# Layer 1 and q computed with the weights as the moving operand in four column groups, w1 in one transfer, GELU's polynomial on GpSimd

## The chip, the cores and the metric

One core of a Trainium2 chip runs the whole kernel. The metric is the device time of one execution in microseconds (us), median of several runs. The execution times quoted are of the fast state unless a state is named. The profiler reports a span, from the first to the last recorded instruction of the kernel. The timed figure is longer than the span, and the difference between the two is "timed minus span". Spans of single runs are known to 0.1 us, so such a difference carries 0.05 us of rounding; for a profiled run the trace has the span to the nanosecond. In the views of the profile, PE is TensorE and PEld its weight loads, DVE is VectorE, ACT ScalarE, POOL GpSimd and SP SyncE. In rows of forty digits, each digit is the busy share of a fortieth of the span, in tenths.

## The reference, cut to what matters

One token, two branches and a gate. All inputs are bfloat16.

```python
q = x @ wq                                  # 576 -> 32 heads x 128
k, v = last 4096 keys of each of 16 caches  # 16 x 4096 x 128 each, 2 heads per cache
a = softmax(q k / sqrt(128)) v @ wo         # -> 576
h = gelu_tanh(x @ w1 + b1)                  # 576 -> 4608
b = h @ w2 + b2                             # -> 576
g = sigmoid(sum(x * gate_w))
out = g * a + (1 - g) * b
```

Some 53.6 MB must be read, most of it k and v, and each byte is used once.

Of the kernel before, what the change touches and what calls it, by code (L numbers as in the profile page):

```python
# [9 lines left out]
FP32 = mybir.dt.float32  # L10
BF16 = mybir.dt.bfloat16
I32 = mybir.dt.int32
ACT = mybir.ActivationFunctionType
ALU = mybir.AluOpType
# [4 lines left out]
def kernel(  # L19
# [15 lines left out]
    nc = tc.nc  # L35

    P = 128
    D = 576
    Hq, Hkv, Dh = 32, 16, 128
# [7 lines left out]
    FH = F // 2  # L47
    NJ = FH // P
    NF = 2 * NJ
    NI = 2 * D // P  # L50
    QH = Hq * Dh // 2
    DH = D // 2
# [153 lines left out]
    const = ctx.enter_context(tc.tile_pool(name="const", bufs=1))  # L206
    big = ctx.enter_context(tc.tile_pool(name="big", bufs=1, side="right"))
    kt_pool = ctx.enter_context(tc.tile_pool(name="kt_pool", bufs=2, side="right"))
    ps_s = ctx.enter_context(tc.tile_pool(name="ps_s", bufs=2, space=bass.MemoryType.PSUM))
    ps_y = ctx.enter_context(tc.tile_pool(name="ps_y", bufs=1, space=bass.MemoryType.PSUM))  # L210
    ps_m = ctx.enter_context(tc.tile_pool(name="ps_m", bufs=2, space=bass.MemoryType.PSUM))


    rows = kt_pool.tile([2, 8192], BF16, name="rows", tag="kt")
    x_row = rows[0:1, 0:D]
    gw_row = rows[0:1, D : 2 * D]
    b2_row = rows[0:1, 2 * D : 3 * D]
    b1_t = rows[0:2, 3 * D : 3 * D + FH]
    xdup = rows[0:1, 3 * D + FH : 5 * D + FH]
    junk_row = rows[0:1, 5 * D + FH : 6 * D + FH]  # L220
# [5 lines left out]

    w1_t = big.tile([P, NI, FH], BF16, name="w1_t", tag="B")
    w1_src = B_w1.rearrange("d (h n) -> (d h) n", h=2).rearrange("(p i) n -> p i n", i=NI)
    for i0, i1 in ((0, 4), (4, NI)):
        nc.sync.dma_start(out=w1_t[:, i0:i1, :], in_=w1_src[:, i0:i1, :])  # L230
    wq_t = big.tile([P, NI, QH], BF16, name="wq_t", tag="A")
    wq_src = A_wq.rearrange("d (h n) -> (d h) n", h=2).rearrange("(p i) n -> p i n", i=NI)
# [10 lines left out]
    for base, pattern, keep in (  # L243
# [13 lines left out]
        out=is0[:], in0=low[:], scalar1=0.0, scalar2=None, op0=ALU.is_equal  # L257
    )
    alt = is0[:, 0 : 2 * NI].rearrange("p (i t) -> p i t", t=2)
    ones = const.tile([P, P], FP32, name="ones")  # L260
    nc.gpsimd.memset(ones[:], 1.0)
    ident = const.tile([P, P], BF16, name="ident")
    make_identity(nc, ident[:])
    RW = 31
    NZ = 512 + 5 * RW + 1 + 64
    zeros = const.tile([P, NZ + 4 * D], BF16, name="zeros")
    nc.gpsimd.memset(zeros[:].bitcast(FP32), 0.0)
    perm = zeros[:, 0:512].rearrange("p (j b l) -> p j b l", j=4, b=4)
    at31 = zeros[:, 512 : 512 + 5 * RW].rearrange("p (a r) -> p a r", a=5)
# [3 lines left out]
        out=perm,  # L273
        in_=perm,
        pattern=[[-64, 2], [-1, 2], [0, 4], [-2, 32]],
        compare_op=ALU.not_equal,
        fill=1.0,
        base=0,
        channel_multiplier=1,
    )  # L280
    nc.gpsimd.affine_select(
        out=at31,
        in_=at31,
        pattern=[[-RW, 5], [-1, RW]],
        compare_op=ALU.not_equal,
        fill=1.0,
        base=0,
        channel_multiplier=1,
# [3 lines left out]
        out=hi5[:],  # L292
        in_=ones[:, 0:5],
        pattern=[[-RW, 5]],
        compare_op=ALU.is_ge,
        fill=0.0,
        base=0,
        channel_multiplier=1,
    )
    nc.gpsimd.affine_select(  # L300
        out=hi5[:],
        in_=hi5[:],
        pattern=[[RW, 5]],
        compare_op=ALU.is_ge,
        fill=0.0,
        base=RW - 1,
        channel_multiplier=-1,
# [4 lines left out]
        out=hi16[:], in0=is0[:, c0 : c0 + 16], scalar1=-SCALE, scalar2=None, op0=ALU.mult  # L312
# [5 lines left out]
        out=row_of[:],  # L318
        in_=row_of[:],
        pattern=[[0, 16], [-1, HB], [0, 2]],  # L320
        compare_op=ALU.not_equal,
        fill=1.0,
        base=0,
        channel_multiplier=1,
# [4 lines left out]
        out=foreign[:],  # L329
        in_=foreign[:],  # L330
        pattern=[[0, P], [-1, HB]],
        compare_op=ALU.not_equal,
        fill=0.0,
        base=0,
        channel_multiplier=1,
# [4 lines left out]
        out=xdup.rearrange("p (d t) -> p d t", t=2),  # L340
        in_=x_row.rearrange("p (d o) -> p d o", o=1).to_broadcast([1, D, 2]),
    )
    xs_ps = ps_m.tile([P, NI, 1], FP32, name="xs_ps", tag="m")
    for i in range(NI):
        nc.tensor.matmul(  # L345
            xs_ps[:, i, :],
            lhsT=xdup[:, i : 2 * D : NI],
            rhs=one_b[0:1, 0:1],
            start=(i == 0),
            stop=(i == NI - 1),  # L350
            skip_group_check=True,
        )
    x2 = const.tile([P, NI, 2], BF16, name="x2")
    nc.vector.tensor_tensor(
        out=x2[:], in0=xs_ps[:].to_broadcast([P, NI, 2]), in1=alt, op=ALU.mult
    )


# [2 lines left out]
        out=junk_row,  # L361
        in0=x_row,
        in1=gw_row,
        scale=1.0,
        scalar=0.0,
        op0=ALU.mult,
        op1=ALU.add,
# [9 lines left out]
    omg = const.tile([P, 1], FP32, name="omg")  # L377
    nc.vector.tensor_scalar(
        out=omg[:], in0=g_t[:], scalar1=-1.0, scalar2=1.0, op0=ALU.mult, op1=ALU.add
    )  # L380
    b2g = const.tile([1, D], FP32, name="b2g")
    nc.vector.tensor_scalar(
        out=b2g[:], in0=b2_row, scalar1=omg[0:1, 0:1], scalar2=None, op0=ALU.mult
    )
    gh = const.tile([P, 1, 5], FP32, name="gh")
# [1 line left out]
        out=gh[:, 0, :], in0=hi5[:], scalar1=g_t[:, 0:1], scalar2=None, op0=ALU.mult  # L387
# [18 lines left out]
    y_add(ones[0:1, 0:1], b2g[0:1, :], start=True)  # L406


    h_ps = ps_m.tile([P, NF], FP32, name="h_ps", tag="m")
    for j in range(NJ):  # L410
        nc.tensor.matmul(
            h_ps[:, j:NF:NJ],
            lhsT=b1_t[:, j:FH:NJ],
            rhs=ident[0:2, 0:2],
            start=(j == 0),
            stop=False,
            skip_group_check=True,
        )
    QZ = 24
    qz_flat = const.tile([P, QZ + 4 * NG * P + 96], BF16, name="qz_flat")  # L420
    nc.gpsimd.memset(qz_flat[:].bitcast(FP32), 0.0)
    for i in range(NI):
        for j in range(NJ):
            nc.tensor.matmul(  # L424
                h_ps[:, j:NF:NJ],
                lhsT=w1_t[:, i, j:FH:NJ],
                rhs=x2[:, i, :],
                start=False,
                stop=(i == NI - 1 and j == NJ - 1),
                skip_group_check=True,  # L430
            )
    hacc = const.tile([P, NF], FP32, name="hacc")
    nc.vector.tensor_copy(out=hacc[:], in_=h_ps[:])  # L433
    z2 = const.tile([P, NF], FP32, name="z2")
    nc.vector.tensor_tensor(out=z2[:], in0=hacc[:], in1=hacc[:], op=ALU.mult)
    C0 = 0.7978845608028654
    poly = const.tile([P, NF], FP32, name="poly")
    nc.vector.tensor_scalar(
        out=poly[:],
        in0=z2[:],  # L440
        scalar1=2.0 * C0 * 0.044715,
# [2 lines left out]
        op1=ALU.add,  # L444
    )
    u_t = const.tile([P, NF], FP32, name="u_t")
    nc.vector.tensor_tensor(out=u_t[:], in0=poly[:], in1=hacc[:], op=ALU.mult)
    e_h = const.tile([P, NF], FP32, name="e_h")
    nc.scalar.activation(out=e_h[:], in_=u_t[:], func=ACT.Exp, scale=-1.0)
    nc.vector.tensor_scalar(out=e_h[:], in0=e_h[:], scalar1=1.0, scalar2=None, op0=ALU.add)  # L450
# [1 line left out]
    nc.vector.reciprocal(out=r_t[:], in_=e_h[:])  # L452
    gt = const.tile([P, NF], BF16, name="gt")
    nc.vector.scalar_tensor_tensor(
        out=gt[:], in0=hacc[:], scalar=omg[:, 0:1], in1=r_t[:], op0=ALU.mult, op1=ALU.mult
    )


    q_ps = ps_m.tile([P, Hq], FP32, name="q_ps", tag="m")
    for i in range(NI):  # L460
        for j in range(Hq // 2):
            nc.tensor.matmul(  # L462
                q_ps[:, j : Hq : Hq // 2],
                lhsT=wq_t[:, i, j * Dh : (j + 1) * Dh],
                rhs=x2[:, i, :],
                start=(i == 0 and j == 0),
                stop=(i == NI - 1 and j == Hq // 2 - 1),
                skip_group_check=True,
            )
    q_b = const.tile([P, Hq], BF16, name="q_b")  # L470
    nc.scalar.copy(out=q_b[:], in_=q_ps[:])
    qj_ps = ps_m.tile([P, 4, NG, 8], FP32, name="qj_ps", tag="m")
    for j in range(4):
        nc.tensor.matmul(
# [293 lines left out]
```

## The kernel before: the parts that the change and the argument touch

All large loads go through SyncE's queue in the order in which they are needed; x, the gate's weights and the two biases, 1 to 9 KB each, go through ScalarE's queue. Two large weights come first, and their buffers are then used again for k, w2 and v.

```python
x_row = rows[0:1, 0:D]
...
b2_row = rows[0:1, 2 * D : 3 * D]
...
w1_t = big.tile([P, NI, FH], BF16, name="w1_t", tag="B")      # NI = 9, FH = 2304
for i0, i1 in ((0, 4), (4, NI)):
    nc.sync.dma_start(out=w1_t[:, i0:i1, :], in_=w1_src[:, i0:i1, :])
wq_t = big.tile([P, NI, QH], BF16, name="wq_t", tag="A")
...                                                            # one transfer
```

In layer 1 and q the weights are the fixed operand: each product first loads a block of 128 x 128 weights and then moves two columns of x past it, which leaves the result spread over 128 partitions.

```python
for i in range(NI):
    for j in range(NJ):                                        # 9 x 18 = 162
        nc.tensor.matmul(h_ps[:, j:NF:NJ], lhsT=w1_t[:, i, j:FH:NJ], rhs=x2[:, i, :], ...)
hacc = const.tile([P, NF], FP32, name="hacc")
nc.vector.tensor_copy(out=hacc[:], in_=h_ps[:])
... # z2 = hacc^2, poly = c1 z2 + c0, u = poly hacc on VectorE, exp on ScalarE,
... # then 1/(1 + e) and the product with (1 - g) on VectorE
for i in range(NI):
    for j in range(Hq // 2):                                   # 9 x 16 = 144
        nc.tensor.matmul(q_ps[:, j : Hq : Hq // 2], lhsT=wq_t[:, i, j * Dh : (j + 1) * Dh],
                         rhs=x2[:, i, :], ...)
nc.scalar.copy(out=q_b[:], in_=q_ps[:])
```

After that come four groups of k (load, transpose on VectorE, scores on TensorE, softmax), four of v, and the two output projections, whose products end the kernel.

## Time and profile before

| | before |
|---|---|
| time, median (lowest to highest of the first three) | 131.68 us (131.63 to 131.78) |
| span of the profiled run | 130.11 us |
| that run's time minus its span | 131.53 - 130.11 = 1.42 us |
| DMA queue, share of 16 engines | 96.5% |
| TensorE, VectorE, GpSimd busy | 79.7, 52.3, 9.2 us |
| last weight packet ends at | 127.50 us |
| instructions as built: TensorE, VectorE, GpSimd | 2211, 60, 47 |

The table says that the transfers fill the span and that the engines do not. The prediction below shows the lines that carry this. This is the start in order of time in the kernel before (start, duration, engine, line, operation, and in brackets how long the engine had been idle and what ended that):

```profile
6.09 0.75 DVE L339 COPY rows<-rows 1x1152 bf16<-1x1152 bf16 x1 [6.09 <-DMA rows<-in_A_x_dram]
7.67 0.75 DVE L360 CUSTOM_DVE_ANT_0 rows<-rows 1x576 bf16<-1x576 bf16 x1 [0.83 <-DMA rows<-in_gate_w_dram]
10.49 1.28 PE L411 MATMUL h_ps<-ident,rows 2*128 2x2 bf16 x18 [1.36 <-DMA rows<-in_B_b_dram]
24.16 0.20 DVE L433 COPY hacc<-h_ps 128x36 f32<-128x36 f32 x1 [11.91 <-PE h_ps L424]
27.00 4.00 PE L462 MATMUL q_ps<-x,wq_t 128*128 128x2 bf16 x144 [2.87 <-DMA wq_t<-in_A_wq_dram]
36.69 4.45 DVE L531 STREAM_TRANSPOSE kt<-k_t 128x4096 f32<-128x4096 f32 x1 [10.47 <-DMA k_t<-in_A_k_cache_dram]
```

The three small inputs x, gate and b1 were there by 6.1, 7.7 and 10.5 us. Layer 1 was summed at 24.16, q's products ran from 27.00, and the first k landed at 36.69.

### The profile page before, as it was taken

How to read it: one execution, taken by the hardware profiler on the slowest of the kernel's cores; microseconds unless marked ns; L12 is line 12 of the kernel's file. 1: busy time of each engine (PE TensorE's matmuls, PEld its weight loads, DVE VectorE, ACT ScalarE, POOL GpSimd, SP SyncE). 2: the span in 40 equal slices, each digit the busy share in tenths (PEclk: the TensorE clock that was granted, in tenths of full speed). 3: DMA queues.
4: the chain of work that ended last, by engine and by line, in shares of the span. 5: the costliest groups of instructions: out<-in, count | busy, mean ns of one | idle time of the engine just before them, and what ended most of it. 6: DMA issues, size and time to landing. Idle time of an engine off the chain costs nothing.

```text
span 130.1 us, 2403 instructions
## 1 busy us (share of the span) xinstructions
PE 79.7 (61%) x1148; PEld 45.6 (35%) x1077; DVE 52.3 (40%) x48; ACT 8.3 (6%) x18; POOL 9.2 (7%) x26
## 2 busy tenths in 40 slices
PE   0037999476003998939918994995300830899573
PEld 0037679375000121201211120595300830855441
DVE  0153000400079959999999995614000020010001
ACT  2000000003000000030003003011000000000001
POOL 7039700000000000000000000000000000000000
PEclk9999999999999999999997799985555555559999
DMA  6999999799899999999899899899899899999980
GB/s 232 427 431 432 476 424 476 344 484 448 373 458 453 403 433 463 393 433 484 373 433 484 383 423 484 357 432 505 368 433 489 363 438 415 442 401 427 413 363 33
DMA packets 2508, 53.75 MB, mean 413 GB/s; under 512 B 286, under 2 KB 290, under 8 KB 580
## 3 DMA queue, kind: packets, MB, share of 16 engines
q1 hardware_dynamic: 2490, 53.61, 96.5%
q8 instruction: 8, 0.13, 0.4%
q10 hardware_dynamic: 10, 0.01, 0.0%
HBM read 53.62 MB, written 0.00 MB: 412 GB/s over the span
## 4 chain that ended last, share of the span: by engine, by line
DMA 52%; DVE 24%; PE 14%; issue 6%; SPq 2%
DMA k_t<-in_A_k_cache_dram 27%; DMA w_t<-in_B_w_dram 25%; DVE kt L531 19%; PE s_ps L553 7%; PE o_ps L640 5%; DVE m L569 3%; DVE pt L602 2%; PE y_ps L396 1%; SPq L684 1%; DVE mr L572 1%; SPq L691 0%; DVE out_row L736 0%; SPq L234 0%; SPq L230 0%; PE mt_ps L578 0%
## 5 line engine op out<-in xcount | busy, mean ns | idle before, releaser
L553 PE MATMUL s_ps<-kt,qz_flat 128*128 128x512 bf16 x128 | 32.9, 414 | 17.2 <-DVE kt L531 10.4
L531 DVE STREAM_TRANSPOSE kt<-k_t 128x4096 f32<-128x4096 f32 x8 | 35.3, 4433 | 12.2 <-DMA k_t<-in_A_k_cache_dram 10.5
L640 PE MATMUL o_ps<-pt,v_t 128*128 128x8 bf16 x512 | 14.2, 168 | 16.6 <-DMA v_t<-in_A_v_cache_dram 14.7
L553 PEld LDWEIGHTS <-qz_flat 128*128 128x128 bf16 x64 | 6.9, 107 | 40.6 <-issue 40.4
L640 PEld LDWEIGHTS <-v_t 128*128 128x128 bf16 x512 | 14.0, 102 | 17.3 <-DMA v_t<-in_A_v_cache_dram 14.9
L424 PEld LDWEIGHTS <-w_t 128*128 128x128 bf16 x162 | 10.3, 167 | 1.8 <-issue 1.8
L424 PE MATMUL h_ps<-x,w_t 128*128 128x2 bf16 x162 | 10.5, 202 | 0.0
L590 ACT ACTIVATE p_t<-s_ps,negm 128x1024 bf16<-128x1024 f32 x4 | 4.5, 1114 | 50.9 <-DVE negm L586 50.9
L396 PE MATMUL y_ps<-w_t,gt 128*1 128x288 bf16 x72 | 6.3, 329 | 1.2 <-DMA w_t<-in_B_w_dram 1.2
L670 DVE RECIPROCAL rg<-mt_ps 128x32 f32<-128x32 f32 x1 | 0.4, 358 | 15.6 <-PE mt_ps L665 15.6
L602 DVE STREAM_TRANSPOSE pt<-p_t 128x1024 bf16<-128x1024 bf16 x4 | 4.9, 1225 | 2.7 <-ACT p_t L590 2.7
L462 PE MATMUL q_ps<-x,wq_t 128*128 128x2 bf16 x144 | 4.0, 166 | 2.9 <-DMA wq_t<-in_A_wq_dram 2.9
L569 DVE TENSOR_REDUCE m<-s_ps 128x1 f32<-128x1024 f32 x4 | 4.8, 1196 | 1.1 <-PE s_ps L553 1.1
L396 PE MATMUL y_ps<-wo_t,ov 128*1 128x288 bf16 x62 | 4.3, 285 | 1.4 <-DMA wo_t<-in_A_wo_dram 1.4
L736 DVE CAST out_row<-y_ps 1x288 bf16<-1x288 f32 x1 | 0.4, 445 | 11.6 <-PE y_ps L396 11.6
L433 DVE COPY hacc<-h_ps 128x36 f32<-128x36 f32 x1 | 0.2, 196 | 11.9 <-PE h_ps L424 11.9
L462 PEld LDWEIGHTS <-wq_t 128*128 128x128 bf16 x144 | 3.9, 104 | 3.0 <-DMA wq_t<-in_A_wq_dram 3.0
L345 PE MATMUL xs_ps<-one_b,rows 1*128 1x1 bf16 x9 | 0.7, 196 | 6.9 <-DVE rows L339 6.9
L396 PEld LDWEIGHTS <-gt 128*1 128x1 bf16 x72 | 3.3, 92 | 3.4 <-issue 1.6
L694 DVE TENSOR_TENSOR om<-o_ps,rgh 128x128 bf16<-128x128 f32 x1 | 0.3, 291 | 8.6 <-PE o_ps L640 8.6
L396 PEld LDWEIGHTS <-ov 128*1 128x1 bf16 x62 | 2.6, 83 | 2.8 <-issue 1.9
L339 DVE COPY rows<-rows 1x1152 bf16<-1x1152 bf16 x1 | 0.7, 748 | 6.1 <-DMA rows<-in_A_x_dram 6.1
(72 smaller groups left out, 35.5 us busy)
## 6 DMA issues: line engine op xcount, KB each, us to landing
k_t<-in_A_k_cache_dram SPq DMA_DIRECT2D x4, 4096.0 KB, 32.1
v_t<-in_A_v_cache_dram SPq DMA_DIRECT2D x4, 4096.0 KB, 22.8
wq_t<-in_A_wq_dram SPq DMA_DIRECT2D x1, 4608.0 KB, 25.8
w_t<-in_B_w_dram SPq DMA_DIRECT2D x1, 2880.0 KB, 14.1
w_t<-in_B_w_dram SPq DMA_DIRECT2D x1, 2592.0 KB, 22.9
w_t<-in_B_w_dram SPq DMA_DIRECT2D x1, 2304.0 KB, 8.1
wo_t<-in_A_wo_dram SPq DMA_DIRECT2D x1, 2304.0 KB
wo_t<-in_A_wo_dram SPq DMA_DIRECT2D x1, 2160.0 KB
```

The costliest lines, as they stand in the source:

```text
L339: nc.vector.tensor_copy(out=xdup.rearrange("p (d t) -> p d t", t=2), in_=x_row.rearrange("p (d o) -> p d o", o=1).to_broadcast([1, D, 2]),)
L396: last = nc.tensor.matmul(y_out[s], lhsT=vec, rhs=row[:, s * DH : (s + 1) * DH], start=start, stop=stop, skip_group_check=True,)
L424: nc.tensor.matmul(h_ps[:, j:NF:NJ], lhsT=w1_t[:, i, j:FH:NJ], rhs=x2[:, i, :], start=False, stop=(i == NI - 1 and j == NJ - 1), skip_grou ...
L462: nc.tensor.matmul(q_ps[:, j : Hq : Hq // 2], lhsT=wq_t[:, i, j * Dh : (j + 1) * Dh], rhs=x2[:, i, :], start=(i == 0 and j == 0), stop=(i ...
L531: lambda: nc.vector.transpose(out=kt[g, f][:].bitcast(FP32), in_=keys.rearrange("p c d -> p (c d)").bitcast(FP32),),
L553: last = nc.tensor.matmul(s_ps[g][:, u * 512 : (u + 1) * 512].rearrange("p (c k) -> p c k", k=32), lhsT=qz(g, j, 2 * f + half), rhs=kv[:, ...
L569: queue("dve", lambda: nc.vector.reduce_max(out=m1[:], in_=s_ps[g][:], axis=AX.X))
L572: lambda: nc.vector.tensor_scalar(out=mr[:], in0=hi16[:], scalar1=m1[:, 0:1], scalar2=None, op0=ALU.mult),
L590: nc.scalar.activation(out=p_t[:].rearrange("p c k -> p (c k)"), in_=s_ps[g][:], func=ACT.Exp, bias=negm[:, 0:1], scale=SCALE, accum_out=s ...
L602: lambda: nc.vector.transpose(out=pt[:, g, :, :].rearrange("p c q -> p (c q)"), in_=p_t[:].rearrange("p c k -> p (c k)"),),
L640: last = nc.tensor.matmul(o_ps[:, 8 * g : 8 * g + 8, 0], lhsT=v_t[g][:, c, :], rhs=pt[:, g, c % 32, 8 * (c // 32) : 8 * (c // 32) + 8], st ...
L684: nc.sync.dma_start(out=wo_t[:, r0:r1, :].rearrange("p r n -> p (r n)"), in_=wo_src[:, 0 : 4 * RW, :].rearrange("h (a r) n -> h a (r n)", ...
```

## The change

Its intent is to shorten the early work on TensorE. With x as the fixed operand (32 columns, of which two are used) and the weights moving in rows of 288 or 512 columns, four products can run side by side, each in a group of 32 columns of the array. The result then lies in a few partitions, as long rows, and has to be copied out and turned. Because the products are few, w1 is taken in one transfer. Three steps of GELU and b2 times (1 - g) go to GpSimd.

```diff
-    b2_row = rows[0:1, 2 * D : 3 * D]
+    b2_row = const.tile([1, D], BF16, name="b2_row")[:]
...
-    for i0, i1 in ((0, 4), (4, NI)):
+    for i0, i1 in ((0, NI),):
         nc.sync.dma_start(out=w1_t[:, i0:i1, :], in_=w1_src[:, i0:i1, :])
...
-    nc.vector.tensor_scalar(
+    nc.gpsimd.tensor_scalar(
         out=b2g[:], in0=b2_row, scalar1=omg[0:1, 0:1], scalar2=None, op0=ALU.mult
...
-    for i in range(NI):
-        for j in range(NJ):
-            nc.tensor.matmul(h_ps[:, j:NF:NJ], lhsT=w1_t[:, i, j:FH:NJ], rhs=x2[:, i, :], ...)
-    nc.vector.tensor_copy(out=hacc[:], in_=h_ps[:])
+    def h_add(g, vec, row, ...):                 # two rows of 288 into column group g
+        ...
+    for i in range(NI):
+        for g in range(4):
+            h_add(g, x2[:, i, :], w1_t[:, i, :], stop=(i == NI - 1))
+    nc.scalar.copy(out=h_sb..., in_=h_ps...)     # 128 x 576
+    nc.vector.transpose(out=early[:, 32 * NJ : 64 * NJ], in_=early[:, 0 : 32 * NJ])
...
-    nc.vector.tensor_tensor(out=z2[:], in0=hacc[:], in1=hacc[:], op=ALU.mult)
+    nc.gpsimd.tensor_tensor(out=halves(z2), in0=hacc, in1=hacc, op=ALU.mult)
...                                              # poly and u_t likewise
-        for j in range(Hq // 2):
-            nc.tensor.matmul(q_ps[...], lhsT=wq_t[:, i, j * Dh : (j + 1) * Dh], rhs=x2[:, i, :], ...)
+        for g in range(4):
+            nc.tensor.matmul(q_ps[32 * g : 32 * g + 32, 0:512], lhsT=x2[:, i, :],
+                             rhs=wq_t[:, i, 512 * g : 512 * (g + 1)], ...)
+    nc.scalar.copy(out=q_rows, in_=q_ps[:, 0:512])
+    for r in range(4):
+        nc.tensor.matmul(qt_ps[:, r:Hq:4], lhsT=q_rows[:, r * Dh : (r + 1) * Dh], rhs=row_is, ...)
```

More of the change, by code (lines that the diff above doesn't have):

```diff
@@ L265 @@
     NZ = 512 + 5 * RW + 1 + 64
-    zeros = const.tile([P, NZ + 4 * D], BF16, name="zeros")
+    XZ = NZ + 4 * D
+    zeros = const.tile([P, XZ + 32 * NI + 8], BF16, name="zeros")
     nc.gpsimd.memset(zeros[:].bitcast(FP32), 0.0)
@@ L275 @@
         pattern=[[-64, 2], [-1, 2], [0, 4], [-2, 32]],
+        compare_op=ALU.not_equal,
+        fill=1.0,
+        base=0,
+        channel_multiplier=1,
+    )
+    x2 = zeros[:, XZ : XZ + 32 * NI].rearrange("p (i m) -> p i m", i=NI)
+    row_is = zeros[:, XZ + 32 * NI : XZ + 32 * NI + 8]
+    nc.gpsimd.affine_select(
+        out=row_is,
+        in_=row_is,
+        pattern=[[-1, 2], [-32, 4]],
         compare_op=ALU.not_equal,
@@ L352 @@
         )
-    x2 = const.tile([P, NI, 2], BF16, name="x2")
     nc.vector.tensor_tensor(
-        out=x2[:], in0=xs_ps[:].to_broadcast([P, NI, 2]), in1=alt, op=ALU.mult
+        out=x2[:, :, 0:2], in0=xs_ps[:].to_broadcast([P, NI, 2]), in1=alt, op=ALU.mult
     )
@@ L406, with h_add @@
     y_add(ones[0:1, 0:1], b2g[0:1, :], start=True)
-    h_ps = ps_m.tile([P, NF], FP32, name="h_ps", tag="m")
-    for j in range(NJ):
-        nc.tensor.matmul(
-            h_ps[:, j:NF:NJ],
-            lhsT=b1_t[:, j:FH:NJ],
-            rhs=ident[0:2, 0:2],
-            start=(j == 0),
-            stop=False,
-            skip_group_check=True,
-        )
+    GW = FH // 4
+    h_ps = ps_s.tile([P, 1024], FP32, name="h_ps", tag="s")
+    def h_add(g, vec, row, start=False, stop=False):
+        for a in range(2):
+            at = g * GW + a * DH
+            nc.tensor.matmul(
+                h_ps[32 * g : 32 * g + 32, 512 * a : 512 * a + DH],
+                lhsT=vec,
+                rhs=row[:, at : at + DH],
+                start=start,
+                stop=stop,
+                skip_group_check=True,
+            )
+    for g in range(4):
+        h_add(g, ident[0:2, 0:32], b1_t, start=True)
     QZ = 24
@@ L422, with halves @@
     for i in range(NI):
-        for j in range(NJ):
-            nc.tensor.matmul(
-                h_ps[:, j:NF:NJ],
-                lhsT=w1_t[:, i, j:FH:NJ],
-                rhs=x2[:, i, :],
-                start=False,
-                stop=(i == NI - 1 and j == NJ - 1),
-                skip_group_check=True,
-            )
-    hacc = const.tile([P, NF], FP32, name="hacc")
-    nc.vector.tensor_copy(out=hacc[:], in_=h_ps[:])
+        for g in range(4):
+            h_add(g, x2[:, i, :], w1_t[:, i, :], stop=(i == NI - 1))
+    early = kt_pool.tile([P, 4096], FP32, name="early", tag="kt")
+    h_sb = early[:, 0 : 32 * NJ].rearrange("p (j m) -> p j m", m=32)
+    h_t = early[:, 32 * NJ : 64 * NJ].rearrange("p (j m) -> p j m", m=32)
+    nc.scalar.copy(
+        out=h_sb.rearrange("p j (a m) -> p j a m", a=2),
+        in_=h_ps[:].rearrange("p (a w) -> p a w", a=2)[:, :, 0:DH].rearrange(
+            "p a (m j) -> p j a m", j=NJ
+        ),
+    )
+    nc.vector.transpose(
+        out=early[:, 32 * NJ : 64 * NJ], in_=early[:, 0 : 32 * NJ]
+    )
+    hacc = h_t[:, :, 0:2].rearrange("p j h -> p h j")
+    def halves(tile_):
+        return tile_[:].rearrange("p (h j) -> p h j", h=2)
     z2 = const.tile([P, NF], FP32, name="z2")
-    nc.vector.tensor_tensor(out=z2[:], in0=hacc[:], in1=hacc[:], op=ALU.mult)
+    nc.gpsimd.tensor_tensor(out=halves(z2), in0=hacc, in1=hacc, op=ALU.mult)
     C0 = 0.7978845608028654
     poly = const.tile([P, NF], FP32, name="poly")
-    nc.vector.tensor_scalar(
+    nc.gpsimd.tensor_scalar(
         out=poly[:],
@@ L446 @@
     u_t = const.tile([P, NF], FP32, name="u_t")
-    nc.vector.tensor_tensor(out=u_t[:], in0=poly[:], in1=hacc[:], op=ALU.mult)
+    nc.gpsimd.tensor_tensor(out=halves(u_t), in0=halves(poly), in1=hacc, op=ALU.mult)
     e_h = const.tile([P, NF], FP32, name="e_h")
@@ L454 @@
     nc.vector.scalar_tensor_tensor(
-        out=gt[:], in0=hacc[:], scalar=omg[:, 0:1], in1=r_t[:], op0=ALU.mult, op1=ALU.mult
+        out=halves(gt), in0=hacc, scalar=omg[:, 0:1], in1=halves(r_t), op0=ALU.mult, op1=ALU.mult
     )
-    q_ps = ps_m.tile([P, Hq], FP32, name="q_ps", tag="m")
+    q_ps = ps_s.tile([P, 1024], FP32, name="q_ps", tag="s")
     for i in range(NI):
-        for j in range(Hq // 2):
+        for g in range(4):
             nc.tensor.matmul(
-                q_ps[:, j : Hq : Hq // 2],
-                lhsT=wq_t[:, i, j * Dh : (j + 1) * Dh],
-                rhs=x2[:, i, :],
-                start=(i == 0 and j == 0),
-                stop=(i == NI - 1 and j == Hq // 2 - 1),
+                q_ps[32 * g : 32 * g + 32, 0:512],
+                lhsT=x2[:, i, :],
+                rhs=wq_t[:, i, 512 * g : 512 * (g + 1)],
+                start=(i == 0),
+                stop=(i == NI - 1),
                 skip_group_check=True,
             )
+    q_rows = early[:, 64 * NJ : 64 * NJ + 256].bitcast(BF16)
+    nc.scalar.copy(out=q_rows, in_=q_ps[:, 0:512])
+    qt_ps = ps_m.tile([P, Hq], FP32, name="qt_ps", tag="m")
+    for r in range(4):
+        nc.tensor.matmul(
+            qt_ps[:, r:Hq:4],
+            lhsT=q_rows[:, r * Dh : (r + 1) * Dh],
+            rhs=row_is,
+            start=(r == 0),
+            stop=(r == 3),
+            skip_group_check=True,
+        )
     q_b = const.tile([P, Hq], BF16, name="q_b")
-    nc.scalar.copy(out=q_b[:], in_=q_ps[:])
+    nc.scalar.copy(out=q_b[:], in_=qt_ps[:])
     qj_ps = ps_m.tile([P, 4, NG, 8], FP32, name="qj_ps", tag="m")
```

## The prediction

> **What bounds the kernel now.** I read the page's forty slices first, then the DMA queue table, then the chain of work that ended last, and last the stretch from the start to 40 us in order of time. In the slices, the row to look at is DMA:
>
> ```profile
> PE   0037999476003998939918994995300830899573
> DVE  0153000400079959999999995614000020010001
> PEclk9999999999999999999997799985555555559999
> DMA  6999999799899999999899899899899899999980
> q1 hardware_dynamic: 2490, 53.61, 96.5%
> q8 instruction: 8, 0.13, 0.4%
> ```
>
> From the second slice to the last but one the 16 DMA engines are busy without a break, while every compute engine has long holes. The main queue alone holds them 96.5% of the span. A fetch of the program itself (the queue called instruction) takes eight packets of 16 KB. The chain says where the end comes from:
>
> ```profile
> 1.65 35.02 DMA k_t<-in_A_k_cache_dram
> 36.69 4.46 DVE kt L531
> 41.19 5.94 PE s_ps L553 x16
> ...
> 94.29 32.93 DMA w_t<-in_B_w_dram
> 127.22 0.04 issue
> 127.27 1.19 PE y_ps L396 x16
> 128.45 0.43 DVE out_row L736
> ```
>
> The middle of that chain names VectorE and TensorE, but that is only when a transfer was issued. Whether the issue mattered is read from the queue's stock. The half of w2 issued at 68.6 us took 22.9 us to land (the table of DMA issues), so at about 91.5. The next load, v's third group, was issued at 79.9 and so stood 11.6 us ahead of running dry. All loads go through one queue in order, so an earlier issue does not make a byte land earlier. Only the number of bytes, the rate, the start of the first and the work after the last set the time. The start of the last stretch is therefore of no weight; its end at 127.22 us is.
>
> In the trace's DMA records, packets of 23040 bytes and more move at 26.95 bytes per ns on one engine. 53.61 MB over 16 engines at that rate is 124.3 us. The first packets start at 1.03 us, so an ideal end is 125.4; the last weight packet ended at 127.5. I put the 2.1 us between (estimates from the same records) to: the engines starting one after the other between 1.03 and 2.0 us, 0.4; slow packets of the first transfer, 0.54 per engine; small pieces and semaphore writes, 0.3; eight instruction packets of 16384 bytes, 0.61 us each at that rate, 4.9 us over 16 engines, 0.3; and an uneven finish:
>
> ```profile
> 125.50:126.00 0.50, 0.50 (x12) 0.36 (x10) 0.00 (x0) 0.00 (x0) 0.00 (x0) 1.00 0.82 336
> 126.00:126.50 0.50, 0.50 (x12) 0.35 (x8) 0.00 (x0) 0.00 (x0) 0.00 (x0) 1.00 0.74 300
> 126.50:127.00 0.50, 0.44 (x8) 0.17 (x3) 0.00 (x0) 0.00 (x0) 0.00 (x0) 1.00 0.72 281
> 127.00:127.50 0.50, 0.23 (x4) 0.17 (x5) 0.00 (x0) 0.00 (x0) 0.00 (x0) 1.00 0.34 129
> ```
>
> The last two columns are the DMA share and GB/s. The idle shares (0.18, 0.26, 0.28, 0.66 of half a microsecond) add to 0.69 us: some engines are done almost 2 us before the slowest.
>
> **What the Trainium skill says.** "DMA: Bandwidth & Descriptors", section Where 436 GB/s comes from, puts the ceiling of the ports into on-chip memory at 435.2 GB/s. The trace agrees: 26.95 times 16 is 431 GB/s, 99% of it, so no reshaping of transfers can win more than about 1% in mid-run. "Runtime: NRT & Kernel Launch", section Instruction fetch mechanics, says that a program streams in by blocks of 256 instructions (16 KiB) over the sequencer's own DMA queue. The trace agrees on the size: 131072 bytes in eight packets; TensorE has 1148 + 1077 = 2225 recorded instructions, 8.7 such blocks. "TensorEngine Tiling (Array Packing)", section Key Properties, says that tiles run loads and products in parallel. The trace agrees for two groups: the y products alternate between two output groups, last 285 ns each by their own record, and yet 40 of them went by in 2.61 us, 65 ns each. Four groups no run here has shown. The same page, section PSUM Bottleneck, warns that tiling does not speed up the copy out; the change adds two such copies.
>
> **The change part by part.** These are the groups that it replaces or leans on:
>
> ```profile
> L424 PE MATMUL h_ps<-x,w_t 128*128 128x2 bf16 x162 | 10.5, 202 | 0.0
> L462 PE MATMUL q_ps<-x,wq_t 128*128 128x2 bf16 x144 | 4.0, 166 | 2.9 <-DMA wq_t<-in_A_wq_dram 2.9
> L433 DVE COPY hacc<-h_ps 128x36 f32<-128x36 f32 x1 | 0.2, 196 | 11.9 <-PE h_ps L424 11.9
> ```
>
> *Layer 1.* 18 + 162 products, each with its own weight load (1.3 + 10.5 us), become 8 + 72 products of 288 columns with x as the fixed side. At 65 ns for each, two groups overlapping, the 72 take 4.7 us; with four, 2.4. They can start only when the whole of w1 has landed, at about 0.8 + 14.1 = 14.9 us, and after the bias row on GpSimd (b2g now queues behind the masks, which end near 14.5; about 1 us, an estimate from VectorE's 0.58 for the same), so near 16. They end near 18.5 to 21 instead of 24.2. Then come a ScalarE copy and a VectorE transpose of 576 columns (4433 ns x 576/4096 = 0.62 us), three GpSimd steps at perhaps 0.3 to 0.4 us (the like one on 16 columns took 257 ns), and the rest as before: near 24, against 26.2. GELU's result is first used at 114.6 us, so all of this lies beside the stream.
>
> *q.* 144 products become 36 of 512 columns plus 4 that turn the rows. wq lands at 27.0 as before. With two groups overlapping 36 x 65 x 512/288 = 4.2 us, with four 2.1, and with none 36 x 227 ns (the 512-wide score product: 16 in 3.63 us) = 8.2. Adding about 1 us for copy and turn and 1.9 for what follows the products today (30.8 to 32.7 us): ready at 32 to 34, at worst 38. It is needed at 41.19, when the first score product starts. So it is hidden even at its worst.
>
> *Buffers.* w1's and wq's room is given back earlier or within a few us of before, so the third and fourth k load queue up with a long stock ahead of them. The new early tile takes the second buffer of kt, which VectorE wants at 41.15; it is free when q is turned, near 31 to 36.
>
> *w1 in one transfer.* Same bytes. Sixteen semaphore writes of 9 ns fall away, one per engine, and rows of 41472 bytes take the place of 18432 and 23040: 0.02 us an engine at the steady rates (26.73 against 26.95). No gain worth a digit.
>
> *The program.* The instruction order of the two kernels shows TensorE's listed rows falling from 2131 to 1643, 488 fewer, or 1.9 blocks. So two of eight instruction packets go: 2 x 0.61 / 16 = 0.08 us off the mean engine, but up to 0.6 us if one of them sat on the engine that finishes last. VectorE loses six early steps of about 0.2 us and gains a transpose, at a time at which it idled.
>
> *Sum.* Off the chain: 0.02 for the transfer, 0.1 to 0.6 for the packets. The tail of 2.9 us after the last landing (1.19 products, 0.43 copy, then the store) does not change. I choose 0.4: 131.68 - 0.4 = 131.3 us.
>
> **The rivals.** *Nothing moves at all* (131.6 to 131.7): the slowest engine may be one without a removed packet, then only 0.0x is won. I give this a good share of the range. *The early work was worth its 15 us of TensorE*, giving 2% or more: for it speaks that the chain passes through TensorE and VectorE up to 94 us; against it the stock of 11.6 us and the unbroken DMA row. *A new wait makes it slower*: VectorE's first transposes wait for q or for the early tile. To cost anything that wait must use up 8.5 us to the first score (41.19 - 32.7) and then 11.6 of stock; I see at most 5. *The clock* could shift: TensorE is granted 0.50 from about 90 to 115 us, and if that fell on the last 16 products their 1.19 us could double, giving 132.9, still within 2%.
>
> **Range and chances.** The lower end takes the whole uneven finish and the packets, 131.68 - 0.9 = 130.8. The upper end is before's highest run, 131.78. Faster by 2% would need 129.05 us, less than the ideal end plus the tail (125.4 + 2.9 + the 1.6 between the span of 130.1 and the 131.68 timed = 129.9), so I give it 0.02. Slower by 2%, 134.3, needs a hole in the stream: 0.02.
>
> **What would show it.** Right: the DMA row still without a hole, the share of the queue about 96 to 97%, instruction packets at six, the wait for k's first group still ending near 36.7 us, TensorE's total down by about 8 to 12 us with no effect, and the last weight packet at 127.0 to 127.4. Wrong: a slice of the DMA row below 7 in mid-run; the first score later than 41.2 us; fewer bytes per ns; or a last landing much under 126.5, meaning that the uneven finish or the start had more in it than I read.

## More of the kernel before

The change's own description calls VectorE's program "60 long". As built here it has 58 instructions, and the one before has 60; I could not settle what the description counted.

## The result, and the profile after

The changed kernel took **132.06 us** (131.96 to 132.14, four runs) against 131.68. The ratio is 1.0028 with a 95% interval of 1.001 to 1.0045: slower by some 0.3%, beyond the noise, and within the 2% that counts as the same. A ratio here is the mean time of one kernel's fast runs over that of the other's in the same rounds, so it is not quite the ratio of the two medians.

The page of the changed kernel, its rows of the slices and of the queues:

```profile
PE   0021229480002998949949945999000840899873
DVE  0024100220069979999999995244000020010001
DMA  7999999899899999999999999899999999999980
q1 hardware_dynamic: 2346, 53.61, 96.6%
q8 instruction: 7, 0.11, 0.4%
```

The DMA row has no hole, as before, and the queue's share is 96.6% where it was 96.5%. TensorE is emptier in the first eight slices (72.7 us busy in all, 79.7 before). The program took seven fetches where it had taken eight. In the chain that ended last (start, duration, what):

```profile
1.86 44.83 DMA k_t<-in_A_k_cache_dram
46.81 4.45 DVE kt L569
...
96.45 30.90 DMA w_t<-in_B_w_dram
127.36 0.04 issue
127.40 1.19 PE y_ps L407 x16
128.59 0.43 DVE out_row L774
```

The same shape, ending 0.13 to 0.14 us later than before at each of the last steps; the tail after the last landing has the same length. The last weight packet ended at 127.62 us (127.50 before). The early work in order of time:

```profile
6.77 0.75 DVE L351 COPY rows<-rows 1x1152 bf16<-1x1152 bf16 x1 [6.77 <-DMA rows<-in_A_x_dram]
10.07 0.75 DVE L371 CUSTOM_DVE_ANT_0 rows<-rows 1x576 bf16<-1x576 bf16 x1 [2.55 <-DMA rows<-in_gate_w_dram]
15.11 0.67 PE L426 MATMUL h_ps<-rows,ident 2*32 2x288 bf16 x8 [3.58 <-DMA rows<-in_B_b_dram]
16.89 1.72 POOL L393 TENSOR_SCALAR b2g<-b_row,omg 1x576 f32<-1x576 bf16 x1
19.72 4.51 PE L426 MATMUL h_ps<-w_t,zeros 128*32 128x288 bf16 x72
26.13 2.13 PE L488 MATMUL q_ps<-wq_t,zeros 128*32 128x512 bf16 x36 [1.90 <-DMA wq_t<-in_A_wq_dram]
27.67 0.28 DVE L480 SCALAR_TENSOR_TENSOR gt<-early,omg,r_t 128x36 bf16<-128x36 f32 x1
37.09 8.77 DVE L569 STREAM_TRANSPOSE kt<-k_t 128x4096 f32<-128x4096 f32 x2 [9.14 <-DMA k_t<-in_A_k_cache_dram]
```

Layer 1's 72 products took 4.51 us, 63 ns each, and q's 36 took 2.13 us, 59 ns each. They end no earlier in the case of layer 1 (24.23 us, 24.13 before), because the small inputs now arrive up to 4.6 us later and b2's step takes 1.72 us on GpSimd. GELU's result is there at 27.95 us (26.22 before). None of it is missed before 41 us. The granted clock of TensorE moved too: in the stretch from 30 to 40 us it was 0.55 where it had been 1.00, and 0.80 instead of 0.87 over the span. The transfers still fill the span, and the last 16 products took 1.19 us as before.

So the span grew by 0.14 us in the profiled runs (130.11 to 130.25), and the time by 0.38. The rest is outside the span: timed minus span is 1.66, 1.74, 1.80 and 1.73 us in the four runs of the changed kernel. In the 51 runs of the kernel before that stood beside the experiments the median is 1.42, and 47 of them lie between 1.37 and 1.48. (Four lie at 1.76 to 2.06. Such single outliers came in other kernels too, also where nothing else moved, and are not explained.)

### The profile page after: what moved, and what is told of

Same layout as the page of the kernel before. It is cut to its first block, busy times and chain, and to the rows that moved or that the text cites. A ratio compares the mean times of both kernels' runs of the same rounds, so it can differ in the third digit from the quotient of the medians.

```text
span 130.3 us, 1959 instructions
## 1 busy us (share of the span) xinstructions
PE 72.7 (56%) x944; PEld 33.3 (26%) x833; DVE 51.7 (40%) x44; ACT 9.5 (7%) x20; POOL 11.7 (9%) x31
## 3 DMA queue, kind: packets, MB, share of 16 engines
q1 hardware_dynamic: 2346, 53.61, 96.6%
## 4 chain that ended last, share of the span: by engine, by line
DMA 58%; DVE 21%; PE 10%; issue 7%; SPq 2%; DVEq 0%
DMA k_t<-in_A_k_cache_dram 34%; DMA w_t<-in_B_w_dram 24%; DVE kt L569 15%; PE o_ps L678 5%; PE s_ps L591 4%; DVE m L607 3%; DVE pt L640 2%; PE y_ps L407 1%; SPq L722 1%; DVE mr L610 1%; SPq L557 0%; SPq L729 0%; DVE out_row L774 0%; SPq L234 0%; PE mt_ps L616 0%
## 5 line engine op out<-in xcount | busy, mean ns | idle before, releaser
L591 PE MATMUL s_ps<-kt,qz_flat 128*128 128x512 bf16 x128 | 33.4, 419 | 19.4 <-DVE kt L569 12.7
L407 PE MATMUL y_ps<-w_t,gt 128*1 128x288 bf16 x72 | 7.2, 363 | 1.2 <-DMA w_t<-in_B_w_dram 1.2
L452 DVE STREAM_TRANSPOSE early<-early 128x576 f32<-128x576 f32 x1 | 0.8, 778 | 10.3 <-ACT early L446 10.3
L426 PE MATMUL h_ps<-w_t,zeros 128*32 128x288 bf16 x72 | 4.5, 445 | 0.0
L488 PE MATMUL q_ps<-wq_t,zeros 128*32 128x512 bf16 x36 | 2.1, 380 | 1.9 <-DMA wq_t<-in_A_wq_dram 1.9
L407 PE MATMUL y_ps<-b2g,ones 1*1 1x288 f32 x4 | 1.1, 657 | 2.9 <-POOL b2g L393 2.9
L426 PE MATMUL h_ps<-rows,ident 2*32 2x288 bf16 x8 | 0.7, 426 | 3.6 <-DMA rows<-in_B_b_dram 3.6
```

The costliest lines, as they stand in the source:

```text
L407: last = nc.tensor.matmul(y_out[s], lhsT=vec, rhs=row[:, s * DH : (s + 1) * DH], start=start, stop=stop, skip_group_check=True,)
L426: nc.tensor.matmul(h_ps[32 * g : 32 * g + 32, 512 * a : 512 * a + DH], lhsT=vec, rhs=row[:, at : at + DH], start=start, stop=stop, skip_gr ...
L452: nc.vector.transpose(out=early[:, 32 * NJ : 64 * NJ], in_=early[:, 0 : 32 * NJ])
L488: nc.tensor.matmul(q_ps[32 * g : 32 * g + 32, 0:512], lhsT=x2[:, i, :], rhs=wq_t[:, i, 512 * g : 512 * (g + 1)], start=(i == 0), stop=(i = ...
L591: last = nc.tensor.matmul(s_ps[g][:, u * 512 : (u + 1) * 512].rearrange("p (c k) -> p c k", k=32), lhsT=qz(g, j, 2 * f + half), rhs=kv[:, ...
```

## The experiments

In the tables and edits below, omg is 1 - g, a small early step on VectorE. Two theories at the start. **A, the start:** a transfer of longer rows begins more slowly and costs a tenth in the span. **B, outside the span:** the length of some engine's program sets the time that is not in the span. For every run the table gives time, mean span, timed minus span (median of its runs), and VectorE's instructions as built (with its waits and branches).

| run | VectorE | time, us | ratio (95%) | span | outside |
|---|---|---|---|---|---|
| before, 51 runs | 60 | 131.68 | | 130.26 | 1.42 |
| changed | 58 | 132.06 | 1.0028 (1.001 to 1.0045) | 130.33 | 1.73 |
| e1 changed, w1 in 4 + 5 | 58 | 131.99 | 1.0026 (1.0013 to 1.0039) | 130.24 | 1.79 |
| e2 before, w1 in one | 60 | 131.71 | 1.0006 (0.9994 to 1.0018) | 130.34 | 1.41 |
| e3 changed, GELU on VectorE | 60 | 131.70 | 1.0009 (0.9992 to 1.0027) | 130.40 | 1.40 |
| e4 as e3, b2 on VectorE | 62 | 131.88 | 1.0017 (1.0005 to 1.0029) | 130.35 | 1.53 |
| e5 changed, 2 more | 60 | 131.73 | 1.0014 (0.9988 to 1.0041) | 130.28 | 1.46 |
| e6 changed, 4 more | 62 | 131.91 | 1.0015 (0.9991 to 1.0039) | 130.38 | 1.56 |
| e7 before, GpSimd 54 | 60 | 131.93 | 1.0010 (0.9986 to 1.0034) | 130.15 | 1.42 and 1.46, 1.94 and 2.08 |
| e8 before, 2 more | 62 | 131.66 | 0.9993 (0.9971 to 1.0015) | 130.15 | 1.50 |
| e9 changed, 1 more | 59 | 131.52 | 0.9980 (0.9961 to 1.0000) | 130.25 | 1.28 |
| e10 changed, 6 more | 64 | 131.72 | 0.9990 (0.9968 to 1.0012) | 130.38 | 1.29 |
| e11 before, TensorE + 1024 | 60 | 139.89 | 1.0534 (1.0490 to 1.0578) | 138.12 | 1.40 |
| e12 before, w1 in 1 + 8 | 60 | 131.67 | 0.9988 (0.9972 to 1.0005) | 130.25 | 1.40 |
| e13 before, 2 fewer | 58 | 132.09 | 1.0029 (1.0017 to 1.0041) | 130.28 | 1.73 |
| e14 before, 1 fewer | 59 | 131.58 | 0.9991 (0.9978 to 1.0004) | 130.28 | 1.30 |
| e15 before, half of v's products | 60 | 131.72 | 1.0007 (0.9995 to 1.0019) | 130.34 | 1.41 |
| e16 changed, w1 in 1 + 8, 1 more | 59 | 131.59 | 0.9995 (0.9982 to 1.0008) | 130.30 | 1.29 |
| e17 changed, 1 fewer | 57 | 132.00 | 1.0025 (1.0004 to 1.0047) | 130.25 | 1.68 |
| e18 changed, 3 more | 61 | 132.04 | 1.0037 (1.0018 to 1.0056) | 130.53 | 1.49 |

### e1 and e2: w1's transfer undone in one kernel, done alone in the other

```diff
# e1, on the changed kernel; e2 is the reverse, on the kernel before
-    for i0, i1 in ((0, NI),):
+    for i0, i1 in ((0, 4), (4, NI)):
```

> The changed kernel with w1 in two transfers again (4 and 5 of the 9 row blocks). Theory A (start): one transfer of 41472-byte rows makes the first packets slow (1.64 us mean against 0.75 + 0.86 for the two), 0.06 MB fewer landed by 5 us, and that puts the last landing 0.11 us later; then this run has first packets as before, x at 6.1 us instead of 6.8, and is 0.1 to 0.2 us faster than the changed kernel (131.9). Theory B (outside the span): timed minus span was 1.42 us before and 1.66 to 1.8 after, and that comes from the programs of the engines, not from transfers; then this run stays at 132.0 to 132.1. Both may hold: 131.9 with 1.7 outside.

> The kernel before with w1 in one transfer, nothing else. Theory A: slow first packets, 131.8 to 131.9. Theory B: 131.7, no change, as only SyncE's program is shorter by one. It also shows whether the small loads (x, gate, b1) come later because of the long rows alone: A expects x at 6.8, gate near 10, b1 near 15 us.

Undoing the transfer won 0.09 us of span (130.24 against 130.33) and left the outside as long as it was; doing it alone cost 0.08 us of span (130.34 against 130.26) and left the outside short. Neither ratio resolves a tenth, but they agree with each other. So do all builds together: the ten with w1 in one transfer have a mean span of 130.35 us (47 runs), the kernel before and the six other builds with 4 + 5 have 130.25 (79 runs). Theory A fits at that size and B holds beside it. The start of e2 shows the other effect of the long rows:

```profile
6.66 0.75 DVE L339 COPY rows<-rows 1x1152 bf16<-1x1152 bf16 x1 [6.66 <-DMA rows<-in_A_x_dram]
9.95 0.75 DVE L360 CUSTOM_DVE_ANT_0 rows<-rows 1x576 bf16<-1x576 bf16 x1 [2.54 <-DMA rows<-in_gate_w_dram]
14.99 1.27 PE L411 MATMUL h_ps<-ident,rows 2*128 2x2 bf16 x18 [3.59 <-DMA rows<-in_B_b_dram]
```

With nothing but w1's rows grown from 18432 and 23040 to 41472 bytes, x, gate and b1 arrive as late as in the changed kernel. It is the long rows that hold them up (e12 below, with two transfers, separates the length of the rows from the number of transfers).

### e3 and e4: GELU's steps, then b2's too, back on VectorE

```diff
-    nc.gpsimd.tensor_tensor(out=halves(z2), in0=hacc, in1=hacc, op=ALU.mult)
+    nc.vector.tensor_tensor(out=halves(z2), in0=hacc, in1=hacc, op=ALU.mult)
...  # poly and u_t likewise; e4: b2g too
```

> The changed kernel with GELU's three steps on VectorE again (VectorE 60 instructions as built instead of 58, GpSimd 51 instead of 54). Theory B with GpSimd's or VectorE's program as the cause: part or all of 0.25 us outside the span comes back, 131.8. Theory A: no change, 132.05. All of the steps lie before 28 us, beside the loads, so within the span nothing should move.

> As e3, and b2 times (1 - g) on VectorE too (VectorE 62 as built, GpSimd 49). Theory B by GpSimd's program: faster than e3 by a little, 131.7 to 131.8. Theory B by VectorE's length (a step past 60): slower than e3. Theory A: 132.05, though layer 1's products can start about 3 us sooner because the bias row no longer waits for GpSimd.

e3 has all of the new products and the single transfer, and with 1.40 us outside it is back at 131.70. That the loss was not in the products is settled by this. e4, with 62 on VectorE, gives part of it back (1.53 us), so fewer instructions on GpSimd is not what helps. The cause could still be ScalarE's program, which had changed in e3 and e4 as well.

### e5 to e8: program lengths alone

```diff
# e5 (changed kernel; e6: range(5)); e8 is range(3) on the kernel before
-    nc.vector.tensor_scalar(
-        out=omg[:], in0=g_t[:], scalar1=-1.0, scalar2=1.0, op0=ALU.mult, op1=ALU.add
-    )
+    for _ in range(3):
+        nc.vector.tensor_scalar(
+            out=omg[:], in0=g_t[:], scalar1=-1.0, scalar2=1.0, op0=ALU.mult, op1=ALU.add
+        )
# e7, on the kernel before
+    for _ in range(7):
+        nc.gpsimd.memset(pad_gpsimd[:], 0.0)
```

> The changed kernel with omg computed three times over on VectorE, so that its program is 60 instructions as built instead of 58; nothing else differs, GpSimd keeps its 54. So far timed minus span was 1.37 to 1.47 us in the three kernels with 60 (before, e2, e3), 1.66 to 1.86 in the two with 58 (the changed one, e1), 1.51 to 1.63 in e4 with 62. Theory B1 (VectorE's program length): 1.40 to 1.45 outside and 131.7 to 131.75 in all, although work was added. Theory B2 (GpSimd's program, 54 in both slow ones): still 1.7 outside, 132.05. Theory B3 (ScalarE's program, 28 in both slow ones): also 1.7.

> As e5 with omg five times over, VectorE's program 62. B1: 1.51 to 1.63 outside as in e4, 131.85. B2 and B3: 1.7.

> The kernel before with seven tiny fills more on GpSimd, 54 instructions as in the changed kernel, VectorE 60 as before. B1: 1.42 outside, 131.68. B2: 1.7 outside, 131.95.

> The kernel before with omg three times over, VectorE's program 62. B1: 1.5 to 1.6 outside, 131.8. B2 and B3: 1.42, 131.68.

Computing omg three times instead of once, work that nobody needs, took four of six runs of the changed kernel from 1.73 to 1.40 to 1.47 us outside. Two had 1.85 and 1.96, outliers of the kind that two of the runs of the kernel before had (1.99 and 2.06). The lengths of GpSimd's and ScalarE's programs were those of the slow kernel, so B2 and B3 fall. e7 is weak alone: two of its four runs were such outliers, the other two had 1.46 and 1.42, where B2 wanted 1.7. In e8 the outside moved by 0.08 us only, and its time did not move (131.66, where 131.8 was expected).

### e9 and e10: 59 and 64 in the changed kernel

> The changed kernel with omg computed twice, VectorE's program 59 instructions as built. If timed minus span falls step by step with the length up to 60, 1.5 to 1.65 us; if 60 is a matter of pairs (an even count), about 1.7; if only 58 is bad, 1.42. The span itself 130.2 to 130.3 in each case.

> The changed kernel with omg seven times over, VectorE's program 64. The three kernels with 62 had a fetch of 8192 bytes of program at about 131.6 us, after the span's end, and 1.5 to 1.6 us outside. If such a fetch is what the length triggers, here too it shows and the outside is 1.5 us or more; if the time goes by some period of the length (58 bad, 60 good, 62 between), it may be back at 1.42 without a fetch.

With 59 the outside fell to 1.27 to 1.35 us in all four runs, the lowest so far, and the time to 131.52, under the kernel before. With 64 it was 1.24 to 1.44. The rule is not monotonic, and not one of even and odd either (60 and 64 are both short, 58 is long).

### e11: 1024 more instructions on TensorE

```diff
-    for j in range(4):
+    for j in [0, 1, 2, 3] * 129:
         nc.tensor.matmul(qj_ps[:, j, :, :]..., lhsT=perm[:, j, :, :]..., rhs=q_b[:], ...)
```

> The kernel before with the four products that spread q repeated 129 times, 1024 instructions more on TensorE, done near 33 to 48 us where TensorE waits for k. That is four more program packets of 16 KB, 12 in place of 8. The step of the prediction (a packet costs up to 0.6 us on the engine that ends last, 0.04 us on the mean): last landing 0.15 to 0.6 us later, 131.85 to 132.3. If the packets are hidden in the uneven finish: 131.68 to 131.75. The first score comes up to 6 us later, which the stock of 11.6 us of queued loads should swallow.

This was meant to price a fetch of the program, and it failed as a test of that, since it broke something else: 139.89 us. Its six runs spread from 137.96 to 140.51, and its profiled run counts as slow by the rule of 1.5% over its own fastest, so I read only what all six share, a loss of over 6 us. The chain of waits in its profile (start, duration, what):

```profile
33.66 3.60 PE qj_ps L474 x128
37.26 3.42 issue
40.68 3.59 PE qj_ps L474 x128
44.27 2.60 issue
46.88 3.60 PE qj_ps L474 x128
50.47 2.60 issue
```

TensorE runs 128 products with their 128 weight loads, 256 instructions, and then stands still for about 3 us with nothing to wait for that the profile shows. The trace has a program packet starting at 38.1, 44.4 and 50.5 us, each about 2.5 us before TensorE goes on. That fits an engine that has run out of program; the profile has no record that says so. So the first score came at 57.8 us instead of 41.2. That is 16.6 us late, more than the stock of 11.6 us that the prediction had worked out, and the DMA row of its page has the hole for it:

```profile
DMA  7999989998999999999995998870899999999981
```

The 5 in slice 22 is a first gap in the loads, the 0 in slice 28 the queue dry. The argument of the stock is borne out from the other side: a delay well above it costs, and that of the changed kernel (first score at 41.59 us, 41.19 before) is far below it. The span grew by 7.2 us on the mean of the three runs that count as fast (7.9 over all six), more than the 5.0 that 16.6 less 11.6 leaves; I did not take that rest apart.

### e12: a short first row

```diff
-    for i0, i1 in ((0, 4), (4, NI)):
+    for i0, i1 in ((0, 1), (1, NI)):
```

> The kernel before with w1 in two transfers of one and eight row blocks, first rows of 4608 bytes in place of 18432 (41472 in the changed kernel). Theory A (long first rows make a slow start): more landed by 5 us than the 1.348 MB of before, x at or before 6.1 us, last landing at or before 127.5, 131.6 or less. If the row length of the start has no effect on the end: 131.68.

1.374 MB had landed by 5 us (1.348 before, 1.283 in the changed kernel), as theory A says, but the mean span is 130.25 against 130.26. Whatever a shorter first row wins at the start is not seen at the end. The small inputs follow the rows: with 4608 bytes first, x was there at 4.76 us (6.09 before), and with rows of 36864 bytes after that, b1 at 13.41 (10.49 before). The kernel before has two transfers as well, so it is the length of the rows that does this.

### e13 and e14: two or one of VectorE's instructions taken away in the kernel before

```diff
# both: b2g; e13: also the polynomial's second step
-    nc.vector.tensor_scalar(
+    nc.gpsimd.tensor_scalar(
```

> The kernel before with two early steps (b2 times 1 - g, and the polynomial's second step) on GpSimd, so that VectorE's program is 58 instructions as built. If the length decides (B1): 1.65 to 1.85 us outside, 131.95 to 132.05 in all, as slow as the changed kernel with none of its products. If 58 is slow only together with the changed kernel's other programs: 1.42 and 131.7.

> The kernel before with b2 times (1 - g) on GpSimd alone, VectorE's program 59. B1: 1.27 to 1.35 outside, 131.5 to 131.6, a little faster than before. Otherwise 1.42.

This is the run that settles it, with e14 as its control, since e13 also adds three instructions to GpSimd and e14 adds two. The kernel before, with its own products and its own transfers, is as slow as the changed one (132.09 against 132.06; outside 1.73 in both) as soon as VectorE's program is 58 long, and with 59 it has the 1.30 us of e9.

### e15: two program fetches fewer, starving nobody

```diff
-        for c in range(NCK):
+        for c in range(0, NCK, 2):
```

> The kernel before with every second value product left out (a wrong result on purpose): 512 instructions fewer on TensorE, two program packets fewer (6 in place of 8), no load changed. The prediction's step: 0.1 to 0.6 us off, span 129.65 to 130.15 against 130.26. If the packets hide in the uneven finish: span 130.2 to 130.3 and outside 1.42, 131.65 to 131.7.

The result is wrong on purpose (half of v is left out; relative error 0.07). The queue of the program on its page:

```profile
q8 instruction: 6, 0.10, 0.3%
```

Six fetches in place of eight, and the span is 130.34 us, not under 130.26. The ratio's interval (0.9995 to 1.0019) leaves room for a gain of 0.07 us at most, less than the 0.1 to 0.6 expected; what lies below that, the run cannot resolve.

### e16: the two good values together

> The changed kernel with w1 in two transfers of one and eight row blocks and omg computed twice (VectorE 59). B1 and A together: span 130.2, outside 1.28, 131.45 to 131.55, about 0.2 us under the kernel before. If the row length of the start does nothing: as e9, 131.52 all the same.

131.59 us, ratio 0.9995: the outside is short as in e9 (1.25 to 1.37), the span is not. e9 and e14 (0.9980 and 0.9991) lie under the kernel before by 0.1 to 0.2%, and none of the three is resolved below 1. A version that clearly beats the kernel before was not found.

### e17 and e18: 57 and 61

```diff
# e17
-    nc.vector.tensor_scalar(
+    nc.gpsimd.tensor_scalar(
         out=gh[:, 0, :], in0=hi5[:], scalar1=g_t[:, 0:1], scalar2=None, op0=ALU.mult
# e18: omg in range(4)
```

> The changed kernel with one more early step (g times the mask of five rows) on GpSimd, VectorE's program 57. If everything up to 58 is slow: 1.7 us outside, 132.0. If 58 is a single bad value, or length goes by odd and even: 1.3 to 1.45, 131.6.

> The changed kernel with omg computed four times, VectorE's program 61. Odd good, even worse: about 1.3, 131.6. Smooth between 60 (1.41) and 62 (1.53): 1.45 to 1.5.

57 behaves like 58 (1.64 to 1.76 us), 61 like 62 (1.47 to 1.61). By length the medians are now 57: 1.68, 58: 1.73 to 1.79, 59: 1.28 to 1.30, 60: 1.40 to 1.46, 61: 1.49, 62: 1.50 to 1.56, 64: 1.29: a step down of some 0.45 us between 58 and 59, and a rise after it. In the traces of all kernels with 61 or more there is one packet of 8192 bytes of program after the end of the span (at 131.55 to 131.76 us with 61 and 62, at 130.39 with 64), and none in those with 57 to 60. So what is fetched after the kernel does depend on the length. But the slow 57 and 58 have no such packet, and no trace shows the instructions that run out there.

The packed traces do hold one more record, which no view prints: when each semaphore (a counter by which engines signal to each other) was updated, also after the last instruction of the kernel. The last thing there is a round of nine updates of semaphore 2. With VectorE at 58 (the changed kernel, e1, e13) its sixth update comes 521 to 530 ns after the fifth, and with 59 or 60 only 97 to 109 ns after it. With 60 the fourth comes 176 to 207 ns after the third, with 58 and 59 only 43 to 64. The round ends 1.87 to 1.88 us after the span with 58, 1.46 to 1.47 with 59 and 1.58 to 1.61 with 60. In 13 of the 14 profiled runs of these lengths timed minus span is this end less 0.17 to 0.18 us (e1: less 0.04). So for 58 to 60 the 0.3 us is seen as one late update in the round that follows the kernel. It doesn't explain 57: e17's round ends at 1.53 us without the long gap, though that run had 1.74 outside. With 61 to 64 the two follow each other less closely. Which engine is late there, and why the length of VectorE's program changes that, stays open.

## Why the prediction was wrong, point by point

**What bounds the kernel: right.** The DMA row without a hole, the queue at 96.6%, 7 us less of TensorE without any gain, and e11's hole once the stock was used up, all say the same.

**The stages of layer 1 and q: hidden, as predicted, with sizes off.** Layer 1 was predicted to end near 18.5 to 21 us and ended at 24.2, since the small inputs came late (e2) and b2's step took 1.72 us where I had put 1; the four products that add this row, 1.1 us more, were not in the estimate. GpSimd's three steps took 0.24, 0.22 and 0.28 us, a little under the guess. q was ready at 30.8 us, before the predicted 32 to 34: its 36 products took the 2.1 us of the case of four groups, but started at 26.1 instead of 27.0, and what follows them took 2.6 us instead of 2.9. VectorE lost five early steps, not six. The first k landed at 37.1 instead of 36.7.

**w1 in one transfer, "no gain worth a digit": off by a sign, and by a tenth of a microsecond.** I compared rates of packets in mid-run (and those rates give 0.05 us an engine, not 0.02). At the start, rows of 41472 bytes went at 25.2 bytes per ns on the mean (24.5 and 26.95 for the two transfers before, 25.8 together), and the span was 0.08 us longer in e2.

**"The program: 0.1 to 0.6 us for the packets": the first step that failed.** One fetch went instead of two, because TensorE's 1762 instructions as built are still 6.9 blocks of 256 (2211, 8.6 blocks, before). The fetches were mis-sized too: the prediction took 0.61 us for each from the rate of the large rows, and the trace has 0.98 to 1.10 us. Yet e15 took two away and won nothing that can be seen. That the packets lie in the slack of the uneven finish is my reading: no run shows them on an engine that ends last. The last weight packet ended at 127.62 us, outside the 127.0 to 127.4 named as a sign of being right.

**"The 1.6 between the span and the timed": the step that carried the miss.** I used the difference of the timed figure and the span as a constant of every kernel, in the bound for a gain of 2% and silently in the sum. The 1.6 itself set the profiled run's span against the median of other runs; that run's own difference is 131.53 - 130.11 = 1.42. And it is not a constant: it went from 1.42 to 1.73 us, because VectorE's program became 58 instructions long. That is 0.31 of the 0.38 us, shown by e5 (length restored, nothing else) and e13 (the length changed with none of the change's products). The other 0.07 is the span, 130.33 against 130.26, about what w1's transfer cost in e2; that the transfer is its cause is likely, not shown. The sum should have read: packets 0, transfer + 0.08, outside + 0.31, which gives 132.07 for the measured 132.06.

**The rivals.** "Nothing moves" was nearest, and a new wait or a slower clock in the last products did not come about: those 16 products took 1.19 us in both kernels. The clock did fall elsewhere (0.55 from 30 to 40 us), where it cost the span nothing that can be seen. That the program's length acts after the last instruction was not among the rivals. The words in the change's description about VectorE's program were the one hint at it, and I did not follow it.

**What the Trainium skill added here.** "Runtime: NRT & Kernel Launch", section The ~15µs preamble/postamble breakdown, lists work that follows a kernel: waiting for all engines and resetting semaphores, about 1.5 us each. The runs agree that there is time after the span that counts, 1.24 to 1.86 us apart from outliers, and the semaphore records fit in kind: in the changed kernel's trace nearly every semaphore from 7 to 255 is updated once between 0.25 and 0.87 us after the span, and semaphore 2 in a round before and after. The sizes differ: 0.6 us for these updates, and 1.88 us for all of it. The records don't name the work.

## What to carry to other kernels

When the queue of transfers is full for the whole span, price early work by the stock of queued bytes: a delay within the stock cost nothing that these runs resolve, and one of 16.6 us against a stock of 11.6 cost 7. Before crediting a change of a few tenths, take the timed figure apart into span and rest, and count each engine's instructions: moving two of them between engines shifted this kernel by 0.3 us without touching its span. Pad such a program by one or two idle instructions to see whether a small loss is the change or only its length.

## What the Trainium skill lacked or had wrong

- "Runtime: NRT & Kernel Launch", sections Instruction fetch mechanics and The ~15µs preamble/postamble breakdown: neither says that the length of one engine's program moves the time after the last instruction. By VectorE's length: 57 and 58, 1.68 to 1.79 us; 59, 1.28 to 1.30; 60, 1.40 to 1.46; 61 and 62, 1.49 to 1.56; 64, 1.29. 1024 more on TensorE (e11, 1.40) show no such effect, nor do seven more on GpSimd in the two undisturbed runs of e7 (1.42 and 1.46).
- The same page, Instruction fetch mechanics, holds fetches to be hidden because instructions are issued more slowly than they are filled. Beside a full load queue TensorE stood still all the same: 256 instructions ran in 3.60 us and the next block came 2.6 to 3.4 us later (e11).
- "TensorEngine Tiling (Array Packing)", section Theoretical Speedup, gives up to 4 times for four groups. Products of 512 columns came to 59 ns each in four groups against 227 ns for whole-array ones of that width, near 4 times; those of 288 columns came to 63 ns in four groups and 65 in two. Their order may be why, and no run tests it: q goes from group to group with each product, layer 1 gives each group two in succession, and in the trace four products start every 216 ns in q and every 240 ns in layer 1.
- "DMA: Bandwidth & Descriptors", section Queues, rings and completion order, describes turns between queues by packet but gives no cost for long rows: with rows of 41472 bytes in the big queue instead of 18432 and 23040, inputs of 1 to 9 KB came 0.6, 2.3 and 4.5 us later (e2).
